# A routed expert layer on one core: the scatters of the tokens' numbers moved behind the load of the last feed-forward weights

## The chip, the cores and the metric

The kernel runs on one core of one Trainium2 chip. The metric is the device time of one launch in microseconds (us). The kernel before was timed three times; a profiled execution of it, taken by the hardware profiler, gives the trace that is read here. PE is TensorE, PEld its weight load, DVE VectorE, ACT ScalarE, POOL GpSimd, SP SyncE.

## The reference

```python
def reference(**kwargs):
    attn_out = _attn_ref(**attn_kwargs)              # (2, 8, 576, 64)
    x = attn_out.transpose(0, 2, 1, 3).reshape(B * S, H * D)   # 1152 tokens x 512
    x = _moe_ref(x=x, **moe_kwargs)                  # top-1 of 8 experts, capacity 288
    return _moe2_ref(x=x, **moe2_kwargs)             # (x w_a) * (x w_b) w_out

def _moe_ref(x, w_gate, w1, w2, capacity):
...
    for i in range(N):
        e = expert_idx[i]
        if counts[e] < capacity:
            disp[e, counts[e]] = x[i]; pos[i] = counts[e]; counts[e] += 1; keep[i] = True
    h = np.maximum(np.einsum('ecd,edf->ecf', disp, w1), 0.0)
    y = np.einsum('ecf,efd->ecd', h, w2)
    for i in range(N):
        if keep[i]:
            out[i] = gate_w[i] * y[expert_idx[i], pos[i]]
```

Attention with a memory term (softmax over 576 positions per head, plus a learned mix with a product against `M_prev`) gives 1152 tokens of 512 numbers. Each token goes to one of 8 experts (w1: 512 to 1024, ReLU, w2: back to 512), and tokens beyond the capacity of an expert become zero. The kept tokens then go through a gated feed-forward of width 1536; a zero token stays zero.

## The kernel before, in words

**Stages.** Attention and gating come first (until about 180 us of the span). The tokens are written, sorted by expert, to the DRAM tensor `xs_d` (line 808, called from `gate5`). The experts are ranked by their counts on the chip, and the kept tokens lie one behind another in `x2`, expert by expert. Experts of high rank are computed with their weights split into a high and a low part, three products per tile (lines 949 to 951, helper `three`); the expert of rank 2 exactly (lines 1446, 1482); those of lower rank with the tokens as weights (`few`, line 1539, with transposes at 1527 and 1548). The feed-forward follows (`forward`): blocks of 512 of its width, A = w_a, B = w_b, O = w_out, `i` = 0, 1, 2; lines 949 to 951 for x A and x B, 1653 and 1656 for their product, 1677 to 1679 for the product with O, 1685 and 1687 for the sum. The last sum of each tile of 128 tokens is followed by a scatter of its rows to `out` (line 808), for which the tile `ids` must say which token each row is.

**Weights.** A load is 1 MB. Expert weights come by `load_block` (line 935) on SP, the feed-forward's by `load_words` (line 972) on SP, two halves per block. The tiles that receive them are `raw`, `raws` and `rawd`; more than one tile has each of these names. A block of a split expert is cast by ACT (`part<-raw`, line 961) and subtracted by DVE (`part<-raw,part`, line 964), each in two halves, before PE may use it. A half of the feed-forward passes ACT line 1349, DVE lines 1353, 1355, 1359, 1363, ACT 961 and DVE 964.

**The tokens' numbers.** `tell` (in `forward`) calls `token_ids`: four small DVE operations (lines 899 to 902) compute for each token the row that it has among the kept ones, `dsi`; ten indirect DMAs on POOL (line 808) write the tokens' numbers, four bytes each, to those rows of the DRAM tensor `id_d`; one DMA on POOL (line 1613) then loads `id_d` into the tile `ids`. In POOL's program order these eleven are between four copies (line 1761) and the scatters to `out`.

**What sets the order.** `Plan.run` simulates the engines with a cost for each piece of work and calls each piece's function when the simulation reaches it; on each engine the instructions then stand in the order of these calls. A piece is added with its engine, its cost, the pieces that it must follow, and a key: among those that could start, the lowest key goes first. For the branch that runs on these inputs (816 rows, 7 experts) the table `WAY_KEYS` adds a number to each key, for "ids" 94.4. The simulation only orders; on the chip an instruction waits for what the tile framework derives from the tiles that it reads and writes. Several branches are built, and the counts choose one on the chip.

```python
            def tell():
                token_ids(key)
                nc.gpsimd.dma_start(out=ids, in_=id_d.rearrange("(t p) o -> p (t o)", p=128))

            self.work("ids", "POOL", 14.0, tell, (), t - 20, late=3.0)
```

Of the kernel before, what the change touches and what calls it, by code (L numbers as in the profile page):

```python
# [196 lines left out]
def fused_kernel(  # L197
# [895 lines left out]
    for b in range(B):  # L1093
        last = b == B - 1
        n = (b + 1) * NP - 1
        G = GROUPS if last else [(0, NT)]
        for i in range(NT):
            t = b * NT + i
# [121 lines left out]
    if FAST:  # L1220
# [17 lines left out]
        def tokens_ahead():  # L1238
# [5 lines left out]
             late=2.0)  # L1244
# [17 lines left out]
    ids = cst.tile([128, NI], I32, name="ids")  # L1262
    FF = w_a.shape[1]
    NI3 = FF // 512
# [12 lines left out]
    class Way:  # L1277
# [329 lines left out]
        def forward(self, W, key, t, before):  # L1607
# [4 lines left out]
                token_ids(key)  # L1612
                nc.gpsimd.dma_start(out=ids, in_=id_d.rearrange("(t p) o -> p (t o)", p=128))

            self.work("ids", "POOL", 14.0, tell, (), t - 20, late=3.0)
            tiles = cut(-(-W // 128))
            for i in range(NI3):
                s_ = slice(512 * i, 512 * i + 512)
                A, Bq, O = ((c, i) for c in "abo")
                A, Bq, O = (("ff", c, i) for c in "abo")  # L1620
# [7 lines left out]
                need = {A: t, Bq: t + (4 * one if i == 0 else one), O: t + 8 * one}  # L1628
                for blk, src in ((A, w_a[:, s_]), (Bq, w_b[:, s_]), (O, w_out[s_, :])):
                    blocks_[blk] = self.wide(blk, src, need[blk], None)  # L1630
                for gi, n in enumerate(tiles):
                    w = min(128 * n, W - c0)
                    c = 12 * (max(256, w) / 2400.0 + 0.013)
# [79 lines left out]
    def cut(T):  # L1713
        n = -(-T // 4)
        return [T // n + (1 if j < T % n else 0) for j in range(n)]
# [60 lines left out]
    def general(exact):  # L1776
# [11 lines left out]
        with room("x2p") as xp:  # L1788
            x2 = xp.tile([128, KD, 2, N + max(256, -(-top // 32) * 32)], F32R, name="x2")
            for kk in range(KD):  # L1790
                nc.gpsimd.memset(x2[:, kk].bitcast(F32), 0.0)
            with room("mp") as mp, room("wp") as wp:
                h_ = mp.tile([128, 4, 2, SW], F32R, name="h_")
                buffers = {"xte": [mp.tile([128, KD, 128], F32, name="xte")],
                           "he": [[t[:, m] for m in range(8)] for t in [mp.tile([128, 8, 128], F32, name="he")]],
                           "xt": [xt0], "h": [[h_[:, m] for m in range(4)] + [h1[:, m] for m in range(4)]]}
                way = Way(wp, x2, 1, buffers)
                way.limited, t = False, 0.0
                for p in range(E):
                    small = exact and LIMITS[p] >= 5  # L1800
                    for c0 in [0] if small else range(0, top, SW):
                        way.big(RANKS[p], c0, 128 if small else min(SW, top - c0), small, t, 1.0,
                                ["xte" if small else "xt", "he" if small else "h"])
                        t += 30.0
                way.plan.run()
            choose(kept, [768, 960, N], forward)
# [41 lines left out]
```

## Time and profile before

| | us |
|---|---|
| three runs | 445.99, 450.18, 450.95 (median 450.18) |
| profiled execution | 448.67 |
| its span in the trace | 446.9 |
| PE busy | 402.1 (90%) |
| DVE busy | 264.5 (59%) |
| ACT busy | 207.1 (46%) |
| POOL busy | 104.8 (23%) |
| mean granted TensorE clock, share of full | 0.963 |

The span is the part of the execution that the trace shows; 1.8 us lie around it. Times in the rows below count from the start of the span. A busy share is a mean over stages with different limits, so what a stretch is worth is read from that stretch. The idle time of an engine before an instruction stands in square brackets behind it, with what ended it.

### The profile page before, as it was taken

How to read it: one execution, taken by the hardware profiler on the slowest of the kernel's cores; microseconds unless marked ns; L12 is line 12 of the kernel's file. 1: busy time of each engine (PE TensorE's matmuls, PEld its weight loads, DVE VectorE, ACT ScalarE, POOL GpSimd, SP SyncE). 2: the span in 40 equal slices, each digit the busy share in tenths (PEclk: the TensorE clock that was granted, in tenths of full speed). 3: DMA queues.
4: the chain of work that ended last, by engine and by line, in shares of the span. 5: the costliest groups of instructions: out<-in, count | busy, mean ns of one | idle time of the engine just before them, and what ended most of it. 6: DMA issues, size and time to landing. Idle time of an engine off the chain costs nothing.

```text
span 446.9 us, 7876 instructions
## 1 busy us (share of the span) xinstructions
PE 402.1 (90%) x2868; PEld 351.3 (79%) x2868; DVE 264.5 (59%) x639; ACT 207.1 (46%) x451; POOL 104.8 (23%) x182
## 2 busy tenths in 40 slices
PE   6789998989799999588759997999999999999993
PEld 6677887967687999477749795889778897778892
DVE  4567775689784675263350014989885859933231
ACT  3767887479785541351250214444635345113010
POOL 8684576057700005126000000000000000000302
PEclk9999999899899969699869999999999999999998
DMA  3679999838980006399898999965530000000101
GB/s 75 150 171 129 248 289 313 189 72 280 238 294 6 1 2 227 96 392 212 184 366 306 345 390 407 407 243 189 165 118 1 0 1 1 0 1 0 73 25 60
DMA packets 59912, 74.48 MB, mean 167 GB/s; under 512 B 33955, under 2 KB 33955, under 8 KB 59856
## 3 DMA queue, kind: packets, MB, share of 16 engines
q1 hardware_dynamic: 58016, 70.48, 52.0%
q0 software_dynamic: 1632, 3.31, 2.2%
q8 instruction: 27, 0.44, 0.4%
q14 instruction: 29, 0.24, 0.2%
q10 hardware_dynamic: 208, 0.01, 0.0%
HBM read 58.75 MB, written 11.64 MB: 158 GB/s over the span
## 4 chain that ended last, share of the span: by engine, by line
PE 37%; DMA 13%; issue 4%; POOL 1%; ACT 1%; DVE 1%; SPq 0%; POOLq 0%
DMA raw<-in_moe_w_dram 11%; PE bank L949 8%; PE bank L950 8%; PE bank L951 8%; PE bank L1677 4%; PE bank L1678 4%; PE bank L1679 4%; DMA rawd<-xs_d 2%; PE bank L1539 1%; POOL out_dram L808 1%; DVE part L964 1%; ACT part L961 0%; PE bank L958 0%; DVE h L1461 0%; PE bank L1548 0%
## 5 line engine op out<-in xcount | busy, mean ns | idle before, releaser
L949 PE MATMUL bank<-x,part 128*128 128x512 f32 (+1 forms) x192 | 66.7, 348 | 0.4 <-ACT x L961 0.4
L950 PE MATMUL bank<-x,part 128*128 128x512 f32 (+1 forms) x192 | 66.6, 347 | 0.0
L808 POOL DMA_INDIRECT out_dram<-c,ids x4 | 3.9, 986 | 195.6 <-DVE c L1687 193.8
L615 ACT ACTIVATE a<-sv,mn 128x128 f32<-128x128 f32 (+4 forms) x72 | 41.9, 584 | 13.9 <-DVE mn L595 12.9
L949 PEld LDWEIGHTS bank<-x,part 128*128 128x128 f32 x192 | 36.1, 188 | 5.0 <-issue 0.6
L950 PEld LDWEIGHTS bank<-x,part 128*128 128x128 f32 x192 | 36.1, 188 | 4.2
L595 DVE CUSTOM_DVE_ANT_0 sv<-psS,mask 128x128 f32<-128x128 f32 (+4 forms) x72 | 34.6, 515 | 7.9 <-PE psS L579 6.2
L630 PE MATMUL psB<-ident,a 128*128 128x128 f32 x200 | 31.7, 285 | 2.0 <-ACT a L615 1.6
L951 PE MATMUL bank<-x,part 128*128 128x512 f32 (+1 forms) x96 | 33.4, 347 | 0.0
L951 PE MATMUL bank<-x,xt 128*128 128x512 f32 (+1 forms) x96 | 33.3, 346 | 0.0
L630 PEld LDWEIGHTS psB<-ident,a 128*128 128x128 f32 x200 | 24.2, 146 | 6.3 <-ACT a L615 3.4
L647 ACT COPY at<-psB 128x512 f32<-128x512 f32 (+2 forms) x48 | 23.8, 512 | 11.1 <-PE psB L630 10.3
L964 DVE TENSOR_TENSOR x<-bank,x 128x160 f32 (+3 forms) x12 | 4.1, 366 | 39.6 <-ACT x L961 39.6
L961 ACT CAST part<-u 128x1024 fp32r<-128x1024 f32 x18 | 18.7, 1050 | 19.1 <-DVE u L1363 15.8
L1653 ACT COPY c<-bank 128x512 f32<-128x512 f32 (+1 forms) x24 | 11.8, 499 | 25.7 <-PE bank L951 21.5
L1656 DVE TENSOR_TENSOR c<-c,bank 128x512 f32<-128x512 f32 (+1 forms) x24 | 13.7, 576 | 16.0 <-PE bank L951 11.0
L961 ACT CAST a<-c 128x512 fp32r<-128x512 f32 (+1 forms) x12 | 6.4, 534 | 35.4 <-DVE c L1656 28.8
L961 ACT CAST part<-raw 128x1024 fp32r<-128x1024 f32 x14 | 14.2, 1049 | 18.0 <-DMA raw<-in_moe_w_dram 18.0
L964 DVE TENSOR_TENSOR part<-raw,part 128x1024 fp32r<-128x1024 f32 x12 | 14.5, 1229 | 11.7 <-ACT part L961 11.7
L808 POOL DMA_INDIRECT xs_d<-x,di x10 | 10.6, 1060 | 40.8 <-DVE ggt L769 35.0
L951 PEld LDWEIGHTS bank<-x,xt 128*128 128x128 f32 x96 | 18.0, 188 | 2.1
L951 PEld LDWEIGHTS bank<-x,part 128*128 128x128 f32 x96 | 18.0, 188 | 2.1
(281 smaller groups left out, 1090.4 us busy)
## 6 DMA issues: line engine op xcount, KB each, us to landing
raw<-in_moe_w_dram SPq DMA_DIRECT2D x16, 1024.0 KB, 8.8
raws<-in_moe_w_dram SPq DMA_DIRECT2D x6, 1024.0 KB, 15.0
rawd<-in_moe_w_dram SPq DMA_DIRECT2D x6, 1024.0 KB, 20.8
xs_d<-h SPq DMA_DIRECT2D x10, 512.0 KB, 4.7
raw<-in_moe_w_b_dram SPq DMA_DIRECT2D x4, 1024.0 KB, 13.9
d<-s SPq DMA_DIRECT2D x14, 288.0 KB, 3.9
rawd<-in_moe_w_a_dram SPq DMA_DIRECT2D x3, 1024.0 KB, 18.9
raws<-in_moe_w_out_dram SPq DMA_DIRECT2D x3, 1024.0 KB, 5.3
```

The costliest lines, as they stand in the source:

```text
L595: nc.vector.tensor_tensor_reduce(out=o, in0=i0, in1=i1, scale=1.0, scalar=3.0e38, op0=ALU.add, op1=ALU.min, accum_out=mn[:M])
L615: nc.scalar.activation(out=st[u, "a"][:M, h, 0:W], in_=sv[:M, 0:W], func=AF.Exp, scale=-1.0, bias=mn[:M], **more)
L630: nc.tensor.transpose(pt[:kr, M * j:M * j + M], a_t[:M, h, 128 * kt:128 * kt + kr], ident[:M, :M])
L647: eng(out=st[n, a, "at"][:, h0:h0 + nh, 0:i + 1, c0:c0 + 128], in_=pt[:, 0:m * 128].rearrange("p (h k m) -> p h k m", h=nh, m=128))
L808: ins = nc.gpsimd.indirect_dma_start(out=out_[:, :], out_offset=bass.IndirectOffsetOnAxis(ap=idx, axis=0), in_=in_, in_offset=None, bounds ...
L949: nc.tensor.matmul(out_, lhsT=wh, rhs=xh, start=first, stop=False)
L950: nc.tensor.matmul(out_, lhsT=wh, rhs=xl, start=False, stop=False)
L951: nc.tensor.matmul(out_, lhsT=wl, rhs=xh, start=False, stop=last)
L961: nc.scalar.copy(out=to, in_=src)
L964: (eng or nc.vector).tensor_tensor(out=to, in0=src, in1=hi, op=ALU.subtract)
L1677: nc.tensor.matmul(o, lhsT=g[:, 0, ts_], rhs=wh[:, m, :], start=m == 0, stop=False)
L1678: nc.tensor.matmul(o, lhsT=g[:, 0, ts_], rhs=wl[:, m, :], start=False, stop=False)
```

## The change

One line is moved within `forward`, and two of its arguments change.

```diff
-            self.work("ids", "POOL", 14.0, tell, (), t - 20, late=3.0)
             tiles = cut(-(-W // 128))
             for i in range(NI3):
...
                 for blk, src in ((A, w_a[:, s_]), (Bq, w_b[:, s_]), (O, w_out[s_, :])):
                     blocks_[blk] = self.wide(blk, src, need[blk], None)
+                if i == NI3 - 1:
+
+                    self.work("ids", "POOL", 14.0, tell, [("ld", O, n) for n in range(2)], t, late=3.0)
                 for gi, n in enumerate(tiles):
```

The piece "ids" now must follow, in the simulation, the loads of the two halves of the last O block, and its key is that of the last block's beginning. It does the same work as before. On PE, ACT, POOL and SP the instructions stand in the same order as before; on DVE four of them move.

DVE at the start of the branch that runs, before: `big`, `dst` and `dsi` are the tiles of `token_ids`, `part` and `raw` belong to a block of the second expert, `u`, `raws` and `rawd` to halves of a feed-forward block.

```order
626 L1359 SCALAR_TENSOR_TENSOR u_4555<-raws_1917,u_4555 128x1024
627 L964 TENSOR_TENSOR part_210<-raw_4557,part_4602 128x1024 x2
628 L899 TENSOR_TENSOR big<-oh,rs 128x80
629 L900 TENSOR_REDUCE dst<-big 128x10
630 L901 TENSOR_TENSOR dst<-dst,pos 128x10
631 L902 TENSOR_TENSOR dsi<-dst,over 128x10
632 L1363 SCALAR_TENSOR_TENSOR u_4555<-raws_1917,u_4555 128x1024
```

DVE at the same place after the change:

```order
626 L1359 SCALAR_TENSOR_TENSOR u_4555<-raws_1917,u_4555 128x1024
627 L964 TENSOR_TENSOR part_210<-raw_4557,part_4602 128x1024 x2
628 L1363 SCALAR_TENSOR_TENSOR u_4555<-raws_1917,u_4555 128x1024
```

The four operations of lines 899 to 902 are gone from here; the rows on either side of them are the same.

DVE in the feed-forward, before: `c` and `a` are tiles of the gated product (lines 1656 and 964), `u` and `raw` halves of later weight blocks.

```order
714 L1656 TENSOR_TENSOR c<-c,bank_2606 128x304
715 L1353 TENSOR_SCALAR u_4556<-u_4556 128x1024
716 L1355 TENSOR_SCALAR u_4556<-u_4556 128x1024
717 L1353 TENSOR_SCALAR u_4555<-u_4555 128x1024
718 L1355 TENSOR_SCALAR u_4555<-u_4555 128x1024
719 L1359 SCALAR_TENSOR_TENSOR u_4555<-raw_209,u_4555 128x1024
```

DVE at the same place after the change (line 1656 is 1658 there):

```order
710 L1658 TENSOR_TENSOR c<-c,bank_2606 128x304
711 L1353 TENSOR_SCALAR u_4556<-u_4556 128x1024
712 L1355 TENSOR_SCALAR u_4556<-u_4556 128x1024
713 L899 TENSOR_TENSOR big<-oh,rs 128x80
714 L900 TENSOR_REDUCE dst<-big 128x10
715 L901 TENSOR_TENSOR dst<-dst,pos 128x10
716 L902 TENSOR_TENSOR dsi<-dst,over 128x10
717 L1353 TENSOR_SCALAR u_4555<-u_4555 128x1024
718 L1355 TENSOR_SCALAR u_4555<-u_4555 128x1024
```

The four operations now stand between the two pairs of lines 1353 and 1355. POOL's ten scatters and its load of `ids` keep their places in POOL's order and wait for `dsi` as before.

## Rows read from the trace of the kernel before

**Rows 1.** Two stretches of the span: busy time per engine, clock, DMA.
```profile
core 0: us, PE busy (x) PEld busy (x) DVE busy (x) ACT busy (x) POOL busy (x), PEclk, DMA share, GB/s
...
180.00:233.00 53.00, 36.33 (x288) 32.85 (x288) 24.70 (x35) 21.02 (x43) 13.73 (x13) 0.84 0.88 248
...
275.00:340.00 65.00, 64.94 (x321) 54.73 (x322) 54.69 (x66) 32.73 (x45) 0.00 (x0) 1.00 0.59 220
```

**Rows 2.** Chain that ended last, in the stretch 190 to 235 us: start, length, what.
```profile
199.49 24.38 DMA raw<-in_moe_w_dram
...
233.09 0.33 PE bank L949
```

**Rows 3.** The same stretches as POOL's scatters, cut finer (columns as in rows 1).
```profile
200.00:203.90 3.90, 3.90 (x35) 2.38 (x34) 3.90 (x7) 2.49 (x7) 2.99 (x4) 1.00 1.05 388
203.90:222.10 18.20, 14.18 (x92) 13.54 (x93) 4.75 (x7) 3.66 (x7) 6.43 (x6) 0.91 0.96 156
```

**Rows 4.** POOL in order of time, 197 to 415 us.
```profile
197.73 1.72 POOL L808 DMA_INDIRECT id_d<-tid,dsi  x1 [15.96 <-DVE dsi L902]
...
212.31 0.91 POOL L808 DMA_INDIRECT id_d<-tid,dsi  x1 [1.06 <-DMA id_d<-tid,dsi]
...
223.49 1.07 POOL L1613 DMA_DIRECT2D ids<-id_d  x1 [10.27 <-DMA id_d<-tid,dsi]
...
414.86 1.03 POOL L808 DMA_INDIRECT out_dram<-c,ids  x1 [190.30 <-DVE c L1687]
```

**Rows 5.** GB/s of all DMA in 40 equal slices of 200 to 226 us.
```profile
GB/s 394 381 381 397 370 403 211 25 79 129 133 132 110 183 221 211 186 107 281 268 312 224 111 25 63 234 259 202 158 95 54 38 154 174 322 397 413 406 413 403
```

**Rows 6.** ACT in order of time: the casts of the second expert's blocks.
```profile
212.44 1.99 ACT L961 CAST part<-raw 128x1024 fp32r<-128x1024 f32 x2 [6.41 <-DMA raw<-in_moe_w_dram]
...
223.90 1.99 ACT L961 CAST part<-raw 128x1024 fp32r<-128x1024 f32 x2 [8.56 <-DMA raw<-in_moe_w_dram]
...
227.33 1.99 ACT L961 CAST part<-rawd 128x1024 fp32r<-128x1024 f32 x2 [0.83 <-ACT h L1458]
```

**Rows 7.** PE in order of time: first and last of each run of products.
```profile
203.74 0.40 PE L949 MATMUL bank<-b,part 128*128 128x288 f32 x1
...
210.01 0.29 PE L951 MATMUL bank<-b,part 128*128 128x288 f32 x1
213.54 0.40 PE L949 MATMUL bank<-b,part 128*128 128x288 f32 x1 [3.24 <-ACT part L961]
...
222.56 0.29 PE L951 MATMUL bank<-b,xt 128*128 128x288 f32 x1
...
229.84 1.93 PE L1539 MATMUL bank<-raws,c 128*32 128x128 f32 x32 [4.16 <-ACT c L961]
...
250.66 1.96 PE L1539 MATMUL bank<-rawd,c 128*32 128x128 f32 x64
```

**Rows 8.** DVE in order of time, at the old and the new place.
```profile
196.54 0.23 DVE L899 TENSOR_TENSOR big<-oh,rs 128x80 f32<-128x80 f32 x1
...
199.75 1.26 DVE L1363 SCALAR_TENSOR_TENSOR u<-rawd,u 128x1024 int32<-128x1024 int32 x1
...
310.30 0.69 DVE L1353 TENSOR_SCALAR u<-u 128x1024 f32<-128x1024 f32 x1
...
322.05 1.22 DVE L964 TENSOR_TENSOR xt<-u,part 128x1024 fp32r<-128x1024 f32 x1
```

**Rows 9.** SP's issues and ACT's reads of the last O block, PE beside them.
```profile
320.45 0.37 SPq L972 DMA_DIRECT2D rawd<-in_moe_w_out_dram  x1
...
325.74 0.37 SPq L972 DMA_DIRECT2D raws<-in_moe_w_out_dram  x1
...
328.24 0.39 PE L951 MATMUL bank<-x,xt 128*128 128x512 f32 x1
...
342.28 1.15 ACT L1349 ACTIVATE u<-raws 128x1024 f32<-128x1024 f32 x1
...
351.39 0.59 ACT L1653 COPY c<-bank 128x512 f32<-128x512 f32 x1
```

## The prediction

> **What bounds the kernel now.** I read by stage first. From 275 us on PE is busy without a break (64.94 of 65 us at clock 1.00) and DVE nearly so (54.69), while from 180 to 233 us PE works only 36.33 of 53 us at clock 0.84, and DMA is busy 88% of the time [rows 1]. So the late stage is bound by PE, and time is to be had in the early one, where the experts' weights arrive. The chain of waits through it is mostly one row: a weight load issued at 199.49 that lands 24.38 us later, after which it goes on to PE's products of the second expert's second layer at 233.09 [rows 2].
>
> Why does a load of 1 MB take 24 us? Cut finer, the stretch 200 to 203.9 us moves 388 GB/s, the stretch 203.9 to 222.1 only 156, with DMA still 96% busy [rows 3]. The slices show a sharp fall after the sixth (203.9 us) and a sharp recovery at the 35th (222.1 us), to 397 and more [rows 5]. POOL's line has the same edges: its first scatter of the tokens' numbers starts at 197.73, its tenth at 212.31, and the load of `ids`, which waits for all ten to land, starts at 223.49 [rows 4]. The loads in flight are large ones; the scatters write four bytes per token. I take it that the scatters slow the loads while they land.
>
> What that costs is seen in ACT and PE. ACT waits 6.41 and 8.56 us for loads of the second expert [rows 6]. PE ends the first block of its first layer at 210.1 and waits 3.24 us for the second; the second's 48 products take 213.54 to 222.7, 9.2 us where the first's took 6.4, as the clock fell and a low part came late; then PE stands until 229.84, and the 64 products there (line 1539) take 3.25 us, where 64 of them take 1.96 at 250.66 [rows 2, 7].
>
> **The change, part by part.** *DVE at the old place.* Four operations go, 0.83 us from 196.54 on [rows 8]. PE's products that run then do not end earlier by that: the block that stops PE at 210.1 waits for a load, not for DVE. Gain 0.
>
> *The scatters at the old place.* Ten indirect DMAs and the load of `ids` leave the stretch. Without them I let the loads run at the 388 GB/s of the rows just ahead. Lost so far are 18.2 us x (388 - 156) = 4.22 MB, which is 10.9 us at 388.
> - The load behind ACT's cast at 212.44: from 203.9 until then the slices carry 13 x 0.65 us at a mean of 154 GB/s [rows 5], 1.31 MB, which is 3.4 us at 388. It lands at 207.3. ACT needs 2.0 us and DVE's second half ends by 210.8; PE takes the first half at 210.1 without waiting and the second a moment later. The 48 products then take 6.4 us and end at 216.5 and not 222.7: 6.2 us gained.
> - The next loads come the full 10.9 us earlier: ACT casts at 213.0 and at 216.4 instead of 223.90 and 227.33 [rows 6]. PE's line 1539 followed the second cast's start by 2.5 us (229.84), so it starts at 218.9; 64 products at full clock take 1.96 us; the second layer starts at 220.9 and not 233.1. Gain 12.2 us, the 6.2 included.
>
> If the loads were no bound at all behind 216.5, PE would have its transposes (1 us), a copy and the 1.96 us left, which gives 220.5 and 12.6 us; if only the first wait went and the second stayed as long, 6.2. I take 12.2, since both ends of the slow stretch fit the scatters to within a slice or two.
>
> *What follows.* Behind 233 us the loads are issued when PE frees their tiles, so they move with PE, and PE is the bound from 275 us on. I carry the 12.2 us through to the end.
>
> *DVE at the new place.* The four operations (0.83 us) stand ahead of the row at 310.30 [rows 8]. What PE needs soonest behind them is the low part ending at 323.27, read by PE at 328.24 [rows 8, 9]: 5.0 us to spare. Cost 0; without that cover 0.83.
>
> *The scatters at the new place.* POOL starts them when `dsi` is done, so at about 311 us of the old clock. The slow stretch began 6.5 us behind `dsi` and lasted 18.2, so here it lies from 318 to 336. SP's last two loads are issued in it, at 320.45 and 325.74 [rows 9]. At 156 GB/s their 2.10 MB take 13.5 us and are in by 334; ACT reads the second at 342.28. That cover is 8 us; gone, ACT stands at this read, and behind it in its order is the evacuation of a PE bank at 351.39. Nothing else is queued behind the scatters on POOL but the scatters to the output, from 414.86 on [rows 4]; `ids` was asked for 26 us after `dsi`, here at 337, which leaves 77 us. On SP the scatters are moved past nearly all of the remaining weight loads, and that is the point. Cost 0.
>
> *Sum.* 446.9 - 12.2 = 434.7 for the span; the profiled execution is 448.67, so 436.5; it lies 1.5 below the median of the three runs, from which I forecast 450.2 - 12.2 = 438.0.
>
> **The rivals.**
>
> *DVE is held by the scatters.* POOL's ten scatters took 197.73 to 213.2, 15.5 us. Beside them line 1363 took 1.26 us, against 1.22 elsewhere for this size of operation (line 964 at 322.05) [rows 8], which speaks against a hold. But at the new place there are operations of another kind, line 1353, which take 0.69 us for the same 1024 elements [rows 8], and no row shows a scatter beside them. If DVE stood for all 15.5 us and the 0.83, less the 5.0 to spare, PE would be 11.3 late: 449.3.
> The Trainium skill (SBUF — State Buffer, "Who interferes with whom") has it that DVE in a two-port mode and a GpSimd instruction shut each other out for a whole instruction. By that rule one of the two would stand here, and no row of this trace shows which; if it is DVE, the sum is the 449.3 just given.
>
> *The scatters are not what slows the loads.* Then nothing is gained, DVE's 0.83 us is hidden, and the time is 450.2. For it: 1152 numbers of four bytes are next to nothing beside 1 MB loads, and SP issues several loads in a row there. Against it: the two edges, and the 397 to 413 GB/s right behind the last scatter with loads still queued [rows 5].
> The Trainium skill (DMA: Bandwidth & Descriptors, "Queues, rings and completion order") says that each DMA engine takes turns between its queues, a packet at a time. By that alone a few small packets cost little and the sum would be nearly 0; the 156 against 388 GB/s [rows 3] do not agree with so small a cost.
>
> *The last weights come too late (slower).* Place: ACT's read at 342.28. If POOL is the one that is held up beside the operations of line 1353, its scatters spread out and the slow stretch outlasts both loads. At 40 GB/s, about the mean of the lowest four slices (25, 25, 38, 54) [rows 5], 2.10 MB take 52.5 us and land at 373. ACT would stand 30.7 us; 8.0 us lie between this read's end (343.43) and ACT's next row (351.39) [rows 9]; PE would lose 22.7 and the change 10.5 net: 460.7. It decides from 362.5 on, the landing at which the loss equals 12.2, a mean rate of 50 GB/s. Against it: the mean in the old stretch was three times that.
>
> **How the numbers follow.** Forecast 0.77; DVE held 0.07; scatters not the cause 0.09; last weights late 0.07. A measurement of this kernel can tell about 1%, 4.5 us, from no change. Faster by more than that is the forecast with any gain from 6.2 to 12.6, and a small part of the second case: 0.78. Within 1%: 449.3 and 450.2, 0.15. Slower: 0.07. The forecast's own range is 433.8 (the lowest of the three runs, 445.99, less 12.2) to 444.0 (450.2 less 6.2). For 8 in 10 the range takes in the held DVE: 433.8 to 449.5.
>
> **What would show it.** Right: in the new profile the loads between 200 and 222 us run near 388 GB/s, ACT's two waits for them nearly vanish, the second layer of the second expert starts near 221, and everything from 275 us on keeps its shape 12 us earlier; POOL's scatters stand near 299 with a dip in GB/s behind them, and no wait of ACT for a load of w_out. Wrong: a dip that stays at 204 to 222 (the loads' own doing); DVE rows beside the scatters longer than 1.22 and 0.69 us, with PE waiting for them; or ACT's line 1349 waiting for the last loads.

## The result and the profile after

| | before | after |
|---|---|---|
| runs, us | 445.99, 447.53, 450.18, 450.95 | 433.70, 434.44, 434.97, 439.19; a fifth, 432.08 |
| median of the first four, us | 448.86 | 434.71 |
| ratio, 95% interval | | 0.9669 [0.9599, 0.9739] |
| profiled execution, us (span) | 448.67 (446.9) | 439.19 (437.4) |

The kernel is faster by 14.2 us. The profiled executions of the kernel after here and of the last kernel in the table below are over 1.5% above those kernels' fastest runs and count as slow, so the ratios leave them out; that of after_again, the kernel after once more, does not. The first scatter to `xs_d`, which ends the attention stage, starts 3.66 us later in this profile than in that of before. This scatter and the last scatter to the output bracket the part of the span in which the moved work lies. POOL in order of time, the kernel before:

```profile
167.16 1.20 POOL L808 DMA_INDIRECT xs_d<-x,di  x1 [35.03 <-DVE ggt L769]
...
441.00 0.91 POOL L808 DMA_INDIRECT out_dram<-d,ids  x1 [1.80 <-DVE d L1687]
```

And the kernel after, with the scatters of the tokens' numbers between:

```profile
170.82 1.20 POOL L808 DMA_INDIRECT xs_d<-x,di  x1 [34.96 <-DVE ggt L769]
...
301.88 1.19 POOL L808 DMA_INDIRECT id_d<-tid,dsi  x1 [116.36 <-DVE dsi L902]
...
328.42 1.07 POOL L1613 DMA_DIRECT2D ids<-id_d  x1 [10.19 <-DMA id_d<-tid,dsi]
...
431.38 0.91 POOL L808 DMA_INDIRECT out_dram<-d,ids  x1 [1.79 <-DVE d L1689]
```

From the first to the last it was 441.00 - 167.16 = 273.84 us and is 431.38 - 170.82 = 260.56: **13.3 us less**, whatever the attention did. Below I call this the bracket. The profile of after_again has 430.81 - 171.58 = 259.23 us, 14.6 less:

```profile
171.58 1.20 POOL L808 DMA_INDIRECT xs_d<-x,di  x1 [35.30 <-DVE ggt L769]
...
430.81 0.91 POOL L808 DMA_INDIRECT out_dram<-d,ids  x1 [1.79 <-DVE d L1689]
```

Two profiles of one kernel thus differ by 1.3 us in the bracket, and differences of that size below are not read. In both, the attention is some 4 us longer than in that of before; whether the change has a part in this no run shows.

Where the 13.3 us came from is in the stretches that answer to [rows 1, 3]; busy time per engine, clock, DMA share and GB/s of the kernel after:

```profile
200.00:203.90 3.90, 3.90 (x33) 3.68 (x31) 3.87 (x5) 2.88 (x8) 0.00 (x0) 1.00 1.04 391
203.90:222.10 18.20, 17.47 (x138) 15.70 (x136) 10.85 (x18) 9.50 (x17) 0.00 (x0) 1.00 1.05 387
180.00:233.00 53.00, 44.44 (x370) 42.05 (x369) 24.52 (x32) 22.40 (x46) 3.44 (x6) 0.90 0.89 321
```

The second row is the old slow stretch: 387 GB/s and not 156, clock 1.00 and not 0.91. The slices of 200 to 226 us, against [rows 5], have neither edge any more:

```profile
GB/s 318 416 403 410 403 397 391 384 391 381 391 388 388 391 381 388 391 384 391 375 388 394 388 381 394 388 378 397 384 378 397 384 378 397 384 384 394 381 381 394
```

ACT's casts of the second expert's blocks, against [rows 6], wait 0.69 and 2.88 us where they waited 6.41 and 8.56:

```profile
210.62 2.00 ACT L961 CAST part<-raw 128x1024 fp32r<-128x1024 f32 x2 [0.69 <-DMA raw<-in_moe_w_dram]
217.53 2.00 ACT L961 CAST part<-raw 128x1024 fp32r<-128x1024 f32 x2 [2.88 <-DMA raw<-in_moe_w_dram]
220.97 1.99 ACT L961 CAST part<-rawd 128x1024 fp32r<-128x1024 f32 x2 [0.83 <-ACT h L1458]
```

And the chain of waits, which in [rows 2] was a load of 24.38 us, has a load of 13.72 us there and goes on to the 64 products and the second layer:

```profile
205.81 13.72 DMA rawd<-in_moe_w_dram
...
223.48 1.96 PE bank L1539 x64
225.43 0.33 PE bank L949
```

At the new place the GB/s of 290 to 345 us (40 slices), the median landing times of w_out's loads and of the scatters, and SP's issue of the last load:

```profile
GB/s 60 0 0 24 250 408 363 426 66 0 0 0 27 0 63 63 259 406 337 108 21 75 134 143 98 250 301 18 0 15 0 0 0 0 0 0 0 0 0 0
...
raws<-in_moe_w_out_dram SPq DMA_DIRECT2D x2, 1024.0 KB, 11.9
...
id_d<-tid,dsi POOLq DMA_INDIRECT x10, 12.4
...
316.15 0.37 SPq L972 DMA_DIRECT2D raws<-in_moe_w_out_dram  x1
```

The dip has moved here (the last slices before it run at 406 and 337 GB/s, then 21 to 143). The last load of w_out is issued at 316.15, lands 11.9 us later, at 328.1, and ACT reads it without a wait:

```profile
331.52 1.18 ACT L1349 ACTIVATE u<-rawd 128x1024 f32<-128x1024 f32 x1 [0.34 <-DVE part L964]
332.66 1.16 ACT L1349 ACTIVATE u<-raws 128x1024 f32<-128x1024 f32 x1
```

### The profile page after: what moved, and what is told of

Its sections match the earlier page's. It is cut to its first block, busy times and chain, and to the rows that moved or that the text cites. A ratio compares the mean times of both kernels' runs of the same rounds, so it can differ in the third digit from the quotient of the medians.

```text
span 437.4 us, 7876 instructions
## 1 busy us (share of the span) xinstructions
PE 401.5 (92%) x2868; PEld 351.8 (80%) x2868; DVE 267.6 (61%) x639; ACT 207.6 (47%) x451; POOL 107.2 (25%) x182
## 4 chain that ended last, share of the span: by engine, by line
PE 67%; DMA 9%; DVE 7%; ACT 7%; issue 6%; POOL 3%; SPq 0%; POOLq 0%; ACTq 0%; DVEq 0%
PE bank L949 8%; PE bank L950 8%; PE bank L951 8%; PE bank L1679 4%; PE bank L1680 4%; PE bank L1681 4%; DMA rawd<-in_moe_w_dram 3%; PE psB L630 3%; PE psS L579 3%; ACT a L615 3%; PE bank L1446 2%; PE psC L730 2%; DMA d<-s 2%; PE bank L1539 2%; PE psB L949 2%
## 5 line engine op out<-in xcount | busy, mean ns | idle before, releaser
L615 ACT ACTIVATE a<-sv,mn 128x128 f32<-128x128 f32 (+4 forms) x72 | 41.8, 583 | 16.6 <-DVE mn L595 15.5
L808 POOL DMA_INDIRECT id_d<-tid,dsi x10 | 13.6, 1361 | 119.1 <-DVE dsi L902 116.4
L647 ACT COPY at<-psB 128x512 f32<-128x512 f32 (+2 forms) x48 | 23.7, 511 | 12.5 <-PE psB L630 12.0
L961 ACT CAST part<-u 128x1024 fp32r<-128x1024 f32 x18 | 18.7, 1050 | 18.2 <-DVE u L1363 14.9
L579 PE MATMUL psS<-d 128*128 128x256 f32 (+2 forms) x56 | 16.3, 367 | 3.5 <-DVE mn L595 1.9
## 6 DMA issues: line engine op xcount, KB each, us to landing
rawd<-in_moe_w_dram SPq DMA_DIRECT2D x6, 1024.0 KB, 14.6
raws<-in_moe_w_out_dram SPq DMA_DIRECT2D x3, 1024.0 KB, 11.9
```

The lines of the kernel that those rows point to most:

```text
L579: nc.tensor.matmul(sc[:M, h, 0:w], lhsT=l_, rhs=r_, start=j == 0, stop=j == 2)
L615: nc.scalar.activation(out=st[u, "a"][:M, h, 0:W], in_=sv[:M, 0:W], func=AF.Exp, scale=-1.0, bias=mn[:M], **more)
L647: eng(out=st[n, a, "at"][:, h0:h0 + nh, 0:i + 1, c0:c0 + 128], in_=pt[:, 0:m * 128].rearrange("p (h k m) -> p h k m", h=nh, m=128))
L808: ins = nc.gpsimd.indirect_dma_start(out=out_[:, :], out_offset=bass.IndirectOffsetOnAxis(ap=idx, axis=0), in_=in_, in_offset=None, bounds ...
L961: nc.scalar.copy(out=to, in_=src)
```

## The experiments

My theory: the scatters, while they land, slow the weight loads that are queued with them. Rivals: the loads' own backlog, or DVE's moved operations (1); a price per burst and not per scatter (2); the load of `ids` with its 1152 short reads (3). On PE, ACT and SP the instructions of every experiment stand in the order of before (SP's fill has another shape in the two with wide fill); DVE and POOL differ only by the edit. Bracket as above, from one profile each. The kernel before was timed anew beside each group of four, and the ratios refer to these medians: 450.40 us for no_scatters, five_and_five, scatters_old_load_new and doubled_old, 452.07 for one_and_nine, spread_512, rows_512 and tripled_new, 451.09 for the other four.

| kernel | scatters at the old place | bracket, us | median, us | ratio to before, interval |
|---|---|---|---|---|
| before | 10 | 273.84 | 448.86 | 1 |
| no_scatters | 0 | 261.10 | 436.39 | 0.9715 [0.9638, 0.9793] |
| one_and_nine | 1 | 266.94 | 443.39 | 0.9800 [0.9718, 0.9881] |
| five_and_five | 5 | 271.86 | 445.43 | 0.9868 [0.9798, 0.9938] |
| scatters_old_load_new | 10 | 274.80 | 450.36 | 1.0015 [0.997, 1.006] |
| doubled_old | 20 | 286.07 | 461.38 | 1.0234 [1.0167, 1.03] |
| spread_512 | 10, 512 bytes apart | 260.69 | 432.29 | 0.9565 [0.9482, 0.9648] |
| spread_64_wide_fill | 10, 64 bytes apart | 262.81 | 437.08 | 0.9672 [0.9601, 0.9744] |
| rows_512 | 10, rows of 512 bytes | 261.44 | 439.14 | 0.9708 [0.963, 0.9785] |
| after (again) | 0, ten new | 259.23 | 438.12 | 0.9705 [0.9633, 0.9776] |
| tripled_new | 0, thirty new | 261.02 | 438.93 | 0.9696 [0.9617, 0.9775] |
| after_spread_512 | 0, ten new, 512 apart | 260.93 | 431.80 | 0.9566 [0.949, 0.9641] |
| after_spread_64_wide_fill | 0, ten new, 64 apart | 262.31 | 436.63 | 0.9625 [0.9535, 0.9716] |

**Are they the cause?** Scatters left out; the load of `ids`, which then waits for none, starts at 182.68 and is out of the stretch too:

```diff
-        for t in range(NTT):
-            M = rows[t % NT]
-            scatter("id" + key, id_d, dsi[:M, t:t + 1], tid[:M, t:t + 1], N)
...
-            nc.gpsimd.memset(far, 2 * N)
+            nc.gpsimd.iota(far, pattern=[[128, NI]], base=0, channel_multiplier=1)
```

> The kernel before with the ten scatters of the tokens' numbers left out at the old place and at the new; DVE's four operations stay at the old place, and the load of ids (of numbers filled in at the start, so the output rows go to other places, as many and as large) stays in POOL's order. Theory (the landing scatters slow the weight loads): the slow stretch behind 204 us is gone, the second expert's second layer starts 11 to 12 us earlier, time 432 to 436, as the kernel after. How far it lies below the kernel after is the price of the scatters at the new place; I expect under 1 us. Rival 1 (the loads' own backlog, or DVE's four operations): 449, the slow stretch stays.

The bracket, by POOL in order of time, is 261.10 us, 12.7 below before, with DVE's four operations still at the old place:

```profile
167.24 1.19 POOL L808 DMA_INDIRECT xs_d<-x,di  x1 [34.01 <-DVE ggt L769]
...
428.34 0.91 POOL L808 DMA_INDIRECT out_dram<-d,ids  x1 [1.80 <-DVE d L1684]
```

The GB/s of 196 to 236 us (40 slices) show no slow stretch:

```profile
GB/s 393 385 385 387 385 387 385 387 389 387 387 387 385 385 385 377 389 391 387 383 389 387 385 385 389 385 383 403 375 391 389 387 385 389 385 381 393 205 61 100
```

Rival 1 is out; the load of `ids` is tested by itself below. The time, 436.39, is just above what I expected. The kernel after lies at 259.23 and 260.56, so its scatters cost nothing that can be seen at the new place.

**How does the price grow?** Twice as many at the old place (the second ten to `ie_d`, made like `id_d`):

```diff
+        for t in range(NTT):
+            M = rows[t % NT]
+            scatter("ie" + key, ie_d, dsi[:M, t:t + 1], tid[:M, t:t + 1], N)
```

> The kernel before with a second set of ten scatters of the same numbers right behind the first, to a tensor that nobody reads. Theory: the price grows with the number of scatters; the slow stretch lasts some 36 us where it was 18.2, the loads lose another 4.2 MB, 10.9 us at 388 GB/s, and the time is 457 to 461. Rival 1 (not the scatters): 449. Rival 2 (a price per burst, not per scatter): 449 to 452.

The bracket grew by 12.2 us and the time came to 461.38, just above what I expected. The slow stretch lasts 32 us and not 18.2 (columns as in [rows 1]):

```profile
208.50:240.50 32.00, 18.10 (x106) 17.00 (x104) 7.98 (x11) 6.29 (x11) 18.07 (x17) 0.77 1.01 153
```

Five or one there, and the others at the new place (`dsj` is a second copy of `dsi`, computed there; for one, both numbers 5 are 1):

```diff
-        for t in range(NTT):
+        for t in range(5):
...
+    def more_ids(key):
+        nc.vector.tensor_tensor(out=dsj, in0=dst, in1=over, op=ALU.add)
+        for t in range(5, NTT):
+            M = rows[t % NT]
+            scatter("id" + key, id_d, dsj[:M, t:t + 1], tid[:M, t:t + 1], N)
```

> The kernel before with five scatters at the old place and five, with the load of ids, at the new one (held there by a small DVE operation of their own). Theory: half the price, a slow stretch of about 9 us, time 440 to 443. Rival 1: 449. Rival 2 (a price per burst): 447 to 449.

> The kernel before with one scatter at the old place and nine, with the load of ids, at the new one. With none at the old place the time was 14 us lower, with five 5. If the price is per scatter but bounded by how long they land: 436 to 440. If it is per burst (one landing time of 12 us, whatever number lands in it): 444 to 447.

Five did not save half: the bracket, 271.86, is only 2.0 us below before, the median 5.0. I missed here; the time lies between what the theory and rival 2 said, and so does the 443.39 of one_and_nine. The slices of 196 to 236 us with five:

```profile
GB/s 391 387 393 379 385 389 387 385 392 125 53 121 195 178 131 113 138 297 199 152 135 45 20 164 381 403 408 399 385 383 389 389 389 385 381 328 389 387 389 399
```

The loads are slow from 205 to 220 us, 15 us and not the 9 that I expected. Then one scatter, 128 numbers of four bytes, cost 266.94 - 261.10 = **5.8 us** by itself. Its slices (196 to 236 us) and its landing:

```profile
GB/s 391 381 387 391 387 385 387 387 389 385 387 129 68 63 109 178 225 258 309 350 397 406 399 377 387 393 387 387 383 354 381 397 328 301 403 389 377 385 395 393
...
id_d<-tid,dsi POOLq DMA_INDIRECT x1, 12.2
```

Issued at 200.72, it lands 12.2 us later, at 212.9; the loads sink at 207 us and are back at 387 GB/s and more after 216. In the kernel before each of the ten takes about as long (median 12.3 us). So the prices 5.8, 10.8, 12.7 and 25.0 us for one, five, ten and twenty (no_scatters as nothing) follow the length of the slow stretch, about 9, 15, 18 and 32 us, more than the number of scatters: those issued close together land side by side, and another ten behind them land later and cost 12.2 again. Rival 2 is half right.

**Is it the load of ids?** It alone moved, held back by a small operation on DVE:

```diff
+            def rest():
+                nc.vector.memset(ids, 2 * N)
+                nc.gpsimd.dma_start(out=ids, in_=id_d.rearrange("(t p) o -> p (t o)", p=128))
```

> The kernel before with only the load of ids (1152 reads of four bytes) moved to the new place, held there by a small DVE operation; the ten scatters stay at the old place. Theory: the scatters carry the price, time 447 to 449; the waits of 0.59 and 1.62 us of PE at 270 and 272 us may go, about 2 us. Rival 3 (the reads of four bytes slow the loads): 435 to 440.

The ratio is 1.0015: no difference, rival 3 is out. The bracket, 274.80, is no shorter either. Of PE's two late waits for loads one stayed, 0.68 us at 273.84.

**What is it in the scatters?** Four bytes still, but to rows 512 bytes apart:

```diff
-        nc.vector.tensor_tensor(out=dsi, in0=dst, in1=over, op=ALU.add)
+        nc.vector.scalar_tensor_tensor(out=dsi, in0=dst, scalar=float(128), in1=over, op0=ALU.mult, op1=ALU.add)
...
-    id_d = drm.tile([NI * 128, 1], I32, name="id_d")
+    id_d = drm.tile([NI * 128 * 128, 1], I32, name="id_d")
```

> The kernel before with the ten scatters at the old place, still of four bytes a token, but to rows 512 bytes apart and not 4 (the row number times 128; the fill at the start and the load of ids use the same spacing). Theory A (the price is that many writes fall on neighbouring addresses): the slow stretch behind 204 us and the one behind the fill at 35 us shrink, time 434 to 440. Theory B (each write of four bytes has its price wherever it falls): 449 to 452, the slow stretch as before.

At the old place, in the order of before, the whole price is gone, and the time, 432.29, is lower than I expected; in the profile the attention is 2.9 us shorter as well. POOL in order of time, with a bracket of 260.69:

```profile
164.31 1.20 POOL L808 DMA_INDIRECT xs_d<-x,di  x1 [33.79 <-DVE ggt L769]
...
194.80 1.72 POOL L808 DMA_INDIRECT id_d<-tid,dsi  x1 [16.29 <-DVE dsi L902]
...
425.00 0.91 POOL L808 DMA_INDIRECT out_dram<-d,ids  x1 [1.79 <-DVE d L1687]
```

The ten scatters run from 194.80 to 209.5, in the midst of the loads, and these keep their rate (slices of 196 to 236 us) but for one slice; the dip from 229 us on comes when the scatters have long landed, and no_scatters has one like it at 233:

```profile
GB/s 385 383 387 387 392 386 380 392 399 371 377 384 384 395 369 382 373 363 391 389 383 387 372 161 377 383 381 389 387 389 381 391 389 322 115 121 391 408 352 406
...
id_d<-tid,dsi POOLq DMA_INDIRECT x10, 5.2
```

They land in 5.2 us and not 12.3 (medians). As many writes, of as few bytes: beside the loads only their distance changed. Theory A holds and B falls.

Rows of 512 bytes to a tensor that nobody reads:

```diff
-            scatter("id" + key, id_d, dsi[:M, t:t + 1], tid[:M, t:t + 1], N)
+            scatter("iw" + key, iw_d, dsi[:M, t:t + 1], ident[:M, 0:128], N)
```

> The kernel before in which the ten scatters at the old place write rows of 512 bytes, 512 apart, to a tensor that nobody reads (ids come from numbers filled in at the start, so the output rows go to other places, as many and as large). As many descriptors, 128 times the bytes, 0.6 MB, which is 1.5 us at 388 GB/s. Theory A (neighbouring addresses): 435 to 440. Theory B (small writes, each with its own price): also 435 to 440. Theory C (the number of descriptors, whatever they carry): 449 or more.

The bracket is 261.44, and the slices of 196 to 236 us show no slow stretch:

```profile
GB/s 399 363 373 403 410 393 391 383 391 377 391 410 393 401 392 397 371 389 389 399 399 380 388 363 381 293 217 389 383 389 397 381 383 391 383 391 379 387 387 389
```

Theory C falls: as many descriptors, which move 0.42 MB, cost next to nothing. (In its profile the attention is 2.4 us longer than in that of before.) With 64 bytes between rows, and the fill at the start in longer pieces:

```diff
-            nc.sync.dma_start(out=id_d.rearrange("(t p) o -> p (t o)", p=128), in_=far)
+            nc.sync.dma_start(out=id_d.rearrange("(p a w) o -> p a (w o)", p=128, a=2),
+                              in_=far[:, None, :].to_broadcast([128, 2, 8 * NI]))
```

> The kernel before, scatters at the old place, with rows 64 bytes apart and the fill in pieces of 288 bytes. If 64 bytes are far enough apart, as 512 were: from the first scatter to xs_d to the last to the output 260 to 262 us, time 430 to 434. If not, the slow stretch is back in part, 265 to 273 us and 437 to 447.

The bracket is 262.81, and the slices of 195 to 235 us again keep their rate while the scatters land:

```profile
GB/s 330 391 404 412 395 391 385 382 384 392 393 390 389 361 379 388 397 365 373 369 379 383 385 391 339 210 353 379 391 383 389 389 387 385 389 389 385 248 51 49
```

So 64 bytes are nearly or quite enough. Bracket and time, 437.08, both lie above what I expected for that case, by 0.8 and 3 us; 0.9 us of the bracket is behind the feed-forward's first product (166.81 us from there to the last scatter, where before has 165.94), far from these scatters, and why is not known.

**Is there a price at the new place?** Two more sets there, to tensors of their own:

> The kernel after with three sets of scatters at the new place in place of one, two of them to tensors that nobody reads. Theory (behind 300 us only two loads are left and PE has slack): the three sets land until about 360 us, the two loads of w_out land later than their reads only if the rate stays under 50 GB/s; time 434 to 437. Rival (the price is also paid there, and one set hides it only just): 440 to 455, with ACT waiting at line 1349 for a load of w_out.

The bracket is 261.02 against 259.23 and 260.56 with one set; the time, 438.93, is above what I expected, but so is that of the kernel after in the next group. This time ACT does wait at its read of the last load, 3.00 us, and PE does not feel it: from the feed-forward's first product (264.35) to the last scatter (430.29) it is 165.94 us, as before the change. ACT's row:

```profile
334.60 1.12 ACT L1357 ACTIVATE u<-raws 128x1024 f32<-128x1024 f32 x1 [3.00 <-DMA raws<-in_moe_w_out_dram]
```

**A version that beats both, and what the fill does.** Three kernels beside each other:

> The kernel after, unchanged, as the measure for the three runs beside it: 433 to 437, 13 to 15 us below the kernel before. From the first scatter to xs_d to the last scatter to the output it should take 260 to 261 us, as its first profile has it (170.82 to 431.38).

> The kernel after with rows of id_d 512 bytes apart (scatters, fill and load). The scatters cost nothing at the new place already, so whatever it gains over the kernel after comes from the fill in the attention. Theory A (the fill of neighbouring four-byte rows slows the loads of the attention): the first scatter to xs_d 3 us earlier, time 430 to 433. Theory B (the attention's time varies by itself): as the kernel after, 433 to 437.

> The kernel after with rows 64 bytes apart, and the fill in 256 pieces of 288 bytes and not 1152 of four. Theory A: the slow stretch behind the fill is gone, and the time is that of the kernel with rows 512 apart or 1 to 2 us lower, 429 to 433. Theory B: 433 to 437.

The kernel after came out at 438.12, above its expectation, with the bracket 259.23, a little below the 260 to 261 expected. With rows 512 apart the four runs lie at 430.41 to 434.38, all below the four of the kernel after (437.20 to 440.13); the bracket, 260.93, is no shorter, and the first scatter to `xs_d` starts at 163.52 and not 171.58, so the gain is in the attention. There the fill of `id_d` (line 417, issued at 34.95) writes 1152 neighbouring numbers. The stretch 38 to 44.5 us, in the kernel before, with rows 512 apart (spread_512) and with the wide fill (spread_64_wide_fill):

```profile
38.00:44.50 6.50, 5.74 (x52) 4.47 (x50) 4.32 (x15) 5.52 (x12) 1.28 (x2) 1.00 0.90 58
```

```profile
38.00:44.50 6.50, 5.73 (x51) 4.39 (x49) 4.32 (x15) 5.59 (x12) 1.32 (x2) 1.00 0.87 260
```

```profile
38.00:44.50 6.50, 6.17 (x55) 4.84 (x54) 3.83 (x13) 5.82 (x14) 1.85 (x3) 1.00 0.88 289
```

58 against 260 GB/s: the same effect without any indirect DMA. With spacing 512 the first scatter to `xs_d` starts at 164.31 and 163.52 us (two kernels), with the close fill between 167.16 and 171.58 in every profile. But with the wide fill, beside which 289 GB/s move, it starts at 165.86 and, behind the change, at 168.29, where the kernel measured 436.63, no clear gain. That the kernel after with 512-byte spacing is faster than the kernel after, run beside it, is measured; spread_512, with the scatters at the old place, is as fast (432.29 against 431.80, in another group). That the fill's dip is what makes the attention longer is not settled.

## Why the prediction was right

I forecast 438.0 us from 450.2; measured are 434.71 from 448.86. The gain was to be 12.2 us; the brackets give 13.3 and 14.6, the medians 14.2, with 11.7 to 18.0 by the interval of the ratio. The time lies near the lower end of my range, 433.8: 1.3 of the 3.3 us by which the forecast is too high come from the median of before, which a fourth run took from 450.18 to 448.86.

- **The scatters slow the loads: right, and shown** by leaving them out, doubling them and spreading them. What I had not seen is on what this rests: as many writes, as small, cost nothing 512 bytes apart, so it is their neighbouring addresses. The rival "not the cause" had this page rule for it: by the Trainium skill (DMA: Bandwidth & Descriptors, "Queues, rings and completion order") each DMA engine takes turns between its queues, a packet at a time; by that alone a few small packets should cost little. The 5.8 us for a single scatter do not agree with so small a cost.
- **Loads at 388 GB/s: right**, 387.
- **The step of 12.2 us: right, within what two profiles differ by.** From the first scatter to `xs_d` to the second layer it was 233.09 - 167.16 = 65.9 us [rows 2] and is 225.43 - 170.82 = 54.6: 11.3 gained; in after_again the second layer starts 53.4 us behind that scatter, 12.5 gained. Less the 3.7 us of longer attention the casts stand at 207.0, 213.9 and 217.3 where I had 207.3, 213.0 and 216.4. The second load still comes 2.88 us late there, 1.38 in after_again.
- **"Behind 233 us the loads move with PE": put at nothing, measured 1.9 us, cause open.** From the second layer to the feed-forward it was 275.06 - 233.09 = 42.0 us and is 265.47 - 225.43 = 40.0 (39.9 in after_again). Before, PE waited for two loads there:

```profile
270.12 1.08 PE L1539 MATMUL bank<-rawd,c 128*32 128x128 f32 x32 [0.59 <-DMA rawd<-in_moe_w_dram]
272.83 1.08 PE L1539 MATMUL bank<-raw,c 128*32 128x128 f32 x32 [1.62 <-DMA raw<-in_moe_w_dram]
275.06 0.47 PE L949 MATMUL bank<-x,part 128*128 128x512 f32 x1 [0.45 <-ACT x L961]
```

After, the same products run through:

```profile
262.05 1.08 PE L1539 MATMUL bank<-rawd,c 128*32 128x128 f32 x32
263.23 1.08 PE L1539 MATMUL bank<-raw,c 128*32 128x128 f32 x32
265.47 0.47 PE L949 MATMUL bank<-x,part 128*128 128x512 f32 x1 [0.45 <-ACT x L961]
```

  The two steps, 11.3 and 1.9 us, make the 13.3, but for rounding. It looks as if the loads were still catching up at 270 us, but the runs do not show it. PE has such a wait also in spread_512 and in tripled_new, where no scatter slowed the loads at the old place, and the stretch takes 41.0 and 41.3 us there:

```profile
256.87 1.08 PE L1539 MATMUL bank<-raw,c 128*32 128x128 f32 x32 [1.36 <-DMA raw<-in_moe_w_dram]
```

```profile
262.12 1.08 PE L1547 MATMUL bank<-raw,c 128*32 128x128 f32 x32 [1.35 <-DMA raw<-in_moe_w_dram]
```

  And scatters_old_load_new, with the whole slow stretch, takes 40.4. So this 1.9 us may be the load of `ids`, a rest of the delay or chance.
- **From 275 us on the same shape: right.** From the feed-forward's first product to the last scatter it was 441.00 - 275.06 = 165.94 us and is 431.38 - 265.47 = 165.91.
- **DVE held: out.** Beside the scatters line 1353 takes what it took [rows 8]; the first of these rows of line 1353 ran beside the scatter at 301.88, the last beside one at 315.97 (POOL's ten took 16.4 us, 301.88 to 318.23, where they had taken 15.5, so POOL was not held long either):

```profile
301.43 0.17 DVE L902 TENSOR_TENSOR dsi<-dst,over 128x10 int32<-128x10 f32 x1
301.52 0.69 DVE L1353 TENSOR_SCALAR u<-u 128x1024 f32<-128x1024 f32 x1
...
311.11 0.68 DVE L1353 TENSOR_SCALAR u<-u 128x1024 f32<-128x1024 f32 x1
...
316.00 0.70 DVE L1353 TENSOR_SCALAR u<-u 128x1024 f32<-128x1024 f32 x1
```

- **Last weights late: out, but closer than I said.** I had 8 us of cover; the load landed at 328.1 and was read at 332.66, 4.6 us. With three sets the cover was gone, and PE still lost nothing (165.94 us against 165.91). My price for this rival stands on a rate of "about 40" GB/s for the four lowest slices of [rows 5]; their mean is 35.5, which would have put the landing later still, at 380 us.
- **A reading that is off.** PE's first block ends at 210.30 (210.01 + 0.29 [rows 7]) and not at 210.1; the 12.2 us do not hang on it.

## What to carry to other kernels

A DMA that writes single words to neighbouring addresses was dear here for what else was in flight: look for a fall in GB/s that begins some 6 us behind its issue and ends within some 3 us of its landing, even if it moves five kilobytes. Put such a DMA where no load is waited for, or, simpler, space its words out: 64 or 512 bytes apart it cost next to nothing at the very place where it had cost 13 us. And before a gain of one or two microseconds is explained, profile the same kernel twice, and look whether the wait that went is also found in a kernel without the supposed cause.

## What the hardware showed that I had not expected

- Ten scatters of four bytes a token to neighbouring rows land in 12.3 us each (median) and take the loads from 388 to 156 GB/s; 512 bytes apart they land in 5.2 us and the loads keep their rate; rows of 512 bytes land in 6.9 us, with no slow stretch either. Why neighbouring writes hold up loads no run shows.
- The Trainium skill (DMA: Bandwidth & Descriptors, "Specifications") gives 512 bytes as the least transfer for full rate and says that below it the DMA engine reads, modifies and writes back. By that rule alone the four-byte writes 512 apart would be as bad as the close ones. The runs do not agree for the loads beside them: bracket 260.69 against 273.84.
- One scatter of 128 words costs nearly half of what ten cost (5.8 of 12.7 us).
- An ordinary DMA does the same: beside the fill of 1152 neighbouring words all DMA moves 58 GB/s for 6.5 us, with the words 512 bytes apart 260.
